# A one-element GpSimd add on the last weight word ahead of its weight sums, and another fixed order list

## The chip, the cores and the metric

The kernel runs on one core of a Trainium2 chip. The metric is the device time of one execution in microseconds (us). Five engines run their own instruction queues side by side: TensorE (PE, matrix products), VectorE (DVE), ScalarE (ACT), GpSimd (POOL) and SyncE (SP, which here only issues DMA transfers). They wait for one another through semaphores.

## The reference, cut to what matters

```python
B, H, S, D = 8, 8, 576, 64          # q and k are scaled by 5.727 and 5.728
scores = 1/np.sqrt(D) * (q_c @ k_c.transpose(...))     # chunks of 64 tokens
attn = softmax(scores, axis=-1)                         # max subtracted, sum + 1e-9
x = (attn @ v_c)  -> [4608 tokens, 512]                 # heads side by side
h = x @ w_in                                            # w_in  [512, 2048]
g = h * (1 / (1 + exp(-1.702 * h)))
out = g @ w_out                                         # w_out [2048, 512]
```

All is float32 in and out, except that the two weights arrive as float64.

## The kernel before

**Tiles.** The 4608 tokens make 36 tiles of 128 rows, and four tiles make one of nine blocks of 512 tokens. The hidden width of 2048 makes 16 slices of 128, each with its own weight word `w_j` (j from 0 to 15), which holds the slice of `w_in` and of `w_out`. A float32 product is made of three matmuls on a high part and a low part of each operand, so each word is kept as two parts, and so are x (`x_h`, `x_l`) and g (`g_h`, `g_l`).

**Weight words.** A word arrives as float64 (`raw_j`, lines 365 and 370: one DMA for `w_in`, one for `w_out`). ACT scales and takes its low bits (`wsc_j` line 374, `wlow_j` line 381), DVE shifts and joins (`wshift_j` line 387, `wj_j` line 394, in a buffer `wtmp` of which there are three), ACT writes the high part (`wh_j`, line 410) and DVE the low part (`w_j`, line 413).

**The plain blocks.** For block n and slice j with g = 16n + j, PE makes the hidden product (`h0_g`, `h_g`, lines 1513 to 1515; for g below 2 in halves, `hh` and `h`, lines 1526 to 1529) into one of two PSUM banks `hp`. ACT takes the gelu (line 1537) and its high part (`gh_g`, line 1538), DVE the low part (`gl_g`, line 1543), which frees the bank. PE then adds four output steps (`o_g_t`, three matmuls each, lines 1553 to 1555). Blocks 0 to 2 run like that.

**The later blocks.** Blocks 3 to 8 go in three pairs by a scheme with seven products in place of eight (`P1` to `P7`, lines 820 to 822). It needs sums of weight words: for each pair p of slices POOL adds the word's two parts (`pa0_p`, `pa_p`: tile `whole`, line 699) and makes four sums of quarters (`psum_p`: tile `sums`, lines 706 to 709). ACT and DVE split these (`phi`, `plo`), a DMA puts them into a DRAM tile `seven` (`pouts`), and the products read them back in pieces (`ld`, lines 807 and 809).

**Attention.** For each tile, or pair of tiles u, PE makes scores (`s_u`), DVE and ACT the softmax, POOL the division (`n_u`, lines 552 and 1323), DVE or PE the transposes (`tq`, `tk`, `et`), and PE the product with v. q and k of the first tiles come by line 470. Tiles 4 and 5 (u = 4) are loaded as `rows`, transposed by PE (line 1259) and copied out by ACT (line 1266) and DVE (line 1269).

**What sets the order.** Every step is entered once with `plan.add`, with its needs. `ORDER` is a fixed list of step names, and `emit` runs the steps in that order, so each engine gets its instructions in the list's order. `need` is only asserted against that list: on the chip an instruction waits for the data and the buffers that it uses, and for nothing else. Before the change `pa0_p` needs `w_15` (`f"w_{NF - 1}"`, NF = 16) in this sense: it stands behind `w_15` in the list, but it reads only the word 2p.

Of the kernel before, what the change touches and what calls it, by code (L numbers as in the profile page):

```python
# [8 lines left out]
F32 = mybir.dt.float32  # L9
# [5 lines left out]
ALU = mybir.AluOpType  # L15
AX = mybir.AxisListType

PE, ACT, DVE, POOL, DMA = "pe", "act", "dve", "pool", "dma"
# [216 lines left out]
def tile_chunk_attention_ffn(  # L235
# [9 lines left out]
    nc = tc.nc  # L245
# [4 lines left out]
    P = 128  # L250
# [3 lines left out]
    NF = DF // P  # L254
# [1381 lines left out]
    def gelu_table():  # L1636
        z = const.tile([P, P], F32, tag="gelu", name="gelu")
        nc.scalar.activation(z[:, :1], ident[:, :1], AF.Gelu_apprx_sigmoid)
# [55 lines left out]
```

## Time and profile before

| what | us |
|---|---|
| median of 3 runs (819.9 to 821.66) | 821.38 |
| the profiled execution | 821.13 |
| its span, first to last instruction | 819.4 |
| outside the span | 1.7 |
| PE busy in the span | 807.3 |
| DVE, ACT, POOL busy | 586.2, 383.5, 91.5 |

The profile was taken on one execution. A timeline row gives the start in us from the span's start, the length in us, the engine, the line, the operation, what it writes and reads, and in brackets the idle time of the engine before it with what ended it. Matmuls are pipelined: a row lasts longer than the distance to the next one.

### The profile page before, as it was taken

The page shows a single profiled execution, that of the slowest core. Times are in us where ns is not written, and L with a number is a line of the kernel's source. Part 1 is how long each engine was busy: PE and PEld are TensorE (multiplying, and loading weights), DVE is VectorE, ACT ScalarE, POOL GpSimd, SP SyncE. Part 2 cuts the span into 40 slices and gives each one's busy share as a digit, 9 for nine tenths or more (in the row PEclk, how much of TensorE's full clock was granted, in tenths as well). Part 3 has the DMA queues.
Part 4 walks back from the last instruction along what each step waited for, and adds up shares of the span by engine and source line. Part 5 has one row for each costly group of instructions (what it writes and reads, how often), then busy time and mean ns, then how long its engine had stood idle before and what let it go on. Part 6 is the DMA issues. An engine that isn't in the chain of part 4 may idle for free.

```text
span 819.4 us, 15635 instructions
## 1 busy us (share of the span) xinstructions
PE 807.3 (99%) x6038; PEld 680.4 (83%) x6038; DVE 586.2 (72%) x865; ACT 383.5 (47%) x603; POOL 91.5 (11%) x82
## 2 busy tenths in 40 slices
PE   7899999999999999999999999999999999999998
PEld 6788878888888888888888888888888888889998
DVE  5788976356475879885698898776887454569852
ACT  5899824244355536423554352422565311267430
POOL 1000170000063661000001010000000000000000
PEclk9999999999999999999999999999999999999999
DMA  9998645353266677767666437686633047673433
GB/s 242 282 297 244 167 129 123 88 128 72 57 182 174 158 199 207 186 173 219 171 172 167 104 92 193 180 211 198 164 104 116 1 130 213 194 207 118 142 92 103
DMA packets 244010, 131.08 MB, mean 160 GB/s; under 512 B 187104, under 2 KB 211680, under 8 KB 243936
## 3 DMA queue, kind: packets, MB, share of 16 engines
q1 hardware_dynamic: 243936, 130.08, 58.6%
q8 instruction: 48, 0.79, 0.4%
q14 instruction: 26, 0.21, 0.1%
HBM read 97.52 MB, written 32.51 MB: 159 GB/s over the span
## 4 chain that ended last, share of the span: by engine, by line
PE 88%; DVE 4%; SPq 3%; ACT 2%; DMA 2%; issue 1%; DVEq 0%; ACTq 0%
PE po L1553 12%; PE po L1555 12%; PE po L1554 12%; PE hp L820 9%; PE hp L822 9%; PE hp L821 9%; PE hp L1515 4%; PE hp L1513 4%; PE hp L1514 4%; SPq L470 2%; PE s L1293 2%; PE x L1367 2%; DMA w<-seven 1%; DVE wtmp L394 1%; PE acc_X L1069 1%; PE acc_X L1068 1%
## 5 line engine op out<-in xcount | busy, mean ns | idle before, releaser
L1553 PE MATMUL po<-w,g_l 128*128 128x512 f32 x448 | 176.8, 395 | 0.6 <-DVE g_l L1543 0.5
L1555 PE MATMUL po<-w,g_h 128*128 128x512 f32 x448 | 174.5, 390 | 0.0
L1554 PE MATMUL po<-w,g_h 128*128 128x512 f32 x448 | 174.5, 389 | 0.0
L1553 PEld LDWEIGHTS po<-w,g_l 128*128 128x128 f32 x448 | 84.1, 188 | 20.1 <-DVE g_l L1543 1.9
L1555 PEld LDWEIGHTS po<-w,g_h 128*128 128x128 f32 x448 | 84.1, 188 | 17.7
L1554 PEld LDWEIGHTS po<-w,g_h 128*128 128x128 f32 x448 | 84.1, 188 | 16.8
L820 PE MATMUL hp<-w,w 128*128 128x512 f32 x224 | 87.6, 391 | 0.3 <-DMA w<-seven 0.2
L1342 DVE STREAM_TRANSPOSE eT<-e 32x512 f32<-32x512 f32 x120 | 84.2, 702 | 4.4 <-POOL e L1323 2.4
L822 PE MATMUL hp<-w,w 128*128 128x512 f32 x224 | 87.2, 389 | 0.0
L821 PE MATMUL hp<-w,w 128*128 128x512 f32 x224 | 87.1, 389 | 0.0
L1323 POOL TENSOR_TENSOR e<-e,r 128x1024 f32<-128x1024 f32 x16 | 31.2, 1953 | 437.8 <-DVE r L1320 365.0
L1513 PE MATMUL hp<-x_l,w 128*128 128x512 f32 x184 | 72.0, 391 | 0.0
L1515 PE MATMUL hp<-x_h,w 128*128 128x512 f32 x184 | 71.6, 389 | 0.0
L1514 PE MATMUL hp<-x_h,w 128*128 128x512 f32 x184 | 71.6, 389 | 0.0
L1543 DVE TENSOR_TENSOR g_l<-hp,g_h 128x512 fp32r<-128x512 f32 (+1 forms) x50 | 33.2, 664 | 51.9 <-ACT g_h L1538 51.8
L1537 ACT ACTIVATE hp<-hp 128x512 f32<-128x512 f32 (+1 forms) x50 | 28.4, 569 | 66.5 <-PE hp L1515 57.3
L820 PEld LDWEIGHTS hp<-w,w 128*128 128x128 f32 x224 | 42.0, 188 | 10.5 <-issue 1.1
L822 PEld LDWEIGHTS hp<-w,w 128*128 128x128 f32 x224 | 42.1, 188 | 8.8
L821 PEld LDWEIGHTS hp<-w,w 128*128 128x128 f32 x224 | 42.1, 188 | 8.6
L820 PE MATMUL hp<-w,pieces 128*128 128x512 f32 x112 | 43.8, 391 | 0.0
L822 PE MATMUL hp<-w,pieces 128*128 128x512 f32 x112 | 43.6, 389 | 0.0
L821 PE MATMUL hp<-w,pieces 128*128 128x512 f32 x112 | 43.6, 389 | 0.0
(237 smaller groups left out, 1558.6 us busy)
## 6 DMA issues: line engine op xcount, KB each, us to landing
w<-seven SPq DMA_DIRECT2D x112, 256.0 KB, 3.3
pieces<-seven SPq DMA_DIRECT2D x56, 256.0 KB, 3.4
seven<-w SPq DMA_DIRECT2D x24, 512.0 KB, 3.8
raw<-in_moe_w_in_dram SPq DMA_DIRECT2D x16, 512.0 KB, 5.9
raw<-in_moe_w_out_dram SPq DMA_DIRECT2D x16, 512.0 KB, 6.3
four<-four_w SPq DMA_DIRECT2D x32, 256.0 KB, 3.2
raw<-in_q_dram SPq DMA_DIRECT2D x208, 32.0 KB, 2.4
raw<-in_k_dram SPq DMA_DIRECT2D x208, 32.0 KB, 2.2
```

What stands on the lines that cost most here:

```text
L820: nc.tensor.matmul(hp, w[:, 0, c], xl[:, c], start=c == 0, stop=False)
L821: nc.tensor.matmul(hp, w[:, 0, c], xh[:, c], start=False, stop=False)
L822: nc.tensor.matmul(hp, w[:, 1, c], xh[:, c], start=False, stop=c == 1)
L1323: nc.gpsimd.tensor_tensor(st["e"], st["e"], bc(st["r"]), op=ALU.mult)
L1342: nc.vector.transpose(st["et"][po : po + 32, :, 32 * a : 32 * a + 32], st["e"][pi : pi + 32, :, 32 * b : 32 * b + 32],)
L1513: nc.tensor.matmul(hp, wh, xl, start=cc == 0, stop=False)
L1514: nc.tensor.matmul(hp, wh, xh, start=False, stop=False)
L1515: nc.tensor.matmul(hp, wl, xh, start=False, stop=cc == NCC - 1)
L1543: nc.vector.tensor_tensor(gl[:, c], hp, gh[:, c].bitcast(F32), op=ALU.subtract)
L1553: nc.tensor.matmul(po, gl[:, c], w[:, 0, :], start=first, stop=False)
L1554: nc.tensor.matmul(po, gh[:, c], w[:, 0, :], start=False, stop=False)
L1555: nc.tensor.matmul(po, gh[:, c], w[:, 1, :], start=False, stop=last)
```

## The change

A new POOL step `gate` adds one element per partition of word 15's low part to itself. The first sums of each pair need `gate` now. And `ORDER` is another list of the same 2693 names and `gate`.

```diff
-        plan.add(POOL, 1.3, rank, lambda: whole(0), need=[w0, f"w_{NF - 1}"], make=e("pa0"), take=["tmp"])
+        plan.add(POOL, 1.3, rank, lambda: whole(0), need=[w0, "gate"], make=e("pa0"), take=["tmp"])
...
+    def gate():
+        t = const.tile([P, 1], F32, tag="gate", name="gate")
+        w = wt[NF - 1][:, 1, 1, :1].bitcast(F32)
+        nc.gpsimd.tensor_tensor(t, w, w, op=ALU.add)
...
+    plan.add(POOL, 0.12, -80, gate, need=[f"w_{NF - 1}"], make="gate")
...
-    "xa_0 xa_1 k_0 k_1 warm q_0 q_1 k_3 tkp_1 q_3 tkp_0 tk_1 tqp_0 tk_0 q_2 tq_0 tqp_1 raw_0 s_0 tq_1 s_1 m_0 k_2 "
```

Since POOL works off its queue in order, all that stands behind `gate` on POOL begins behind word 15's low part. POOL at that place, before (the names are those of above with the word, pair or tile and a buffer number):

```order
L1323 TENSOR_TENSOR e_6_1019<-e_6_1019,r_6_1061 128x1024
L699 TENSOR_TENSOR whole_2_1301<-w_4_664 128x512
L699 TENSOR_TENSOR whole_2_1301<-w_5_716 128x512
L699 TENSOR_TENSOR whole_0_1383<-w_0_289 128x512
L699 TENSOR_TENSOR whole_0_1383<-w_1_448 128x512
L706 TENSOR_TENSOR sums_2_1400<-whole_2_1301 128x256
```

and now:

```order
L1323 TENSOR_TENSOR e_6_1009<-e_6_1009,r_6_1054 128x1024
L1639 TENSOR_TENSOR gate_1318<-w_15_1312 128x1
L699 TENSOR_TENSOR whole_2_1391<-w_4_667 128x512
L699 TENSOR_TENSOR whole_0_1398<-w_0_305 128x512
L699 TENSOR_TENSOR whole_0_1398<-w_1_446 128x512
L699 TENSOR_TENSOR whole_2_1391<-w_5_727 128x512
L706 TENSOR_TENSOR sums_2_1439<-whole_2_1391 128x256
```

The same four adds stand there in another order, with `gate` ahead of them. The sums of pair 0, which stood right behind those of pair 2, now stand behind two divisions (`n_8` and `n_10`).

DVE around the last three words, before (`eT` and `qkT` are transposes of the attention, L387 and L394 shift and join, L413 is the low part of a word, L1543 the low part of g):

```order
L394 ISA wtmp_14_1150<-raw_14_911,wtmp_14_1150 128x2048
L413 TENSOR_TENSOR w_13_1174<-wtmp_13_1140,w_13_1174 128x2x512
L1342 STREAM_TRANSPOSE eT_6_1101<-e_6_1019 32x16x32 x2
L413 TENSOR_TENSOR w_14_1206<-wtmp_14_1150,w_14_1206 128x2x512
L387 TENSOR_SCALAR wtmp_15_1241<-raw_15_1067 128x1024
L1543 TENSOR_TENSOR g_l_12_1224<-hp_12_1186,g_h_12_1223 128x512
L394 ISA wtmp_15_1241<-raw_15_1067,wtmp_15_1241 128x2048
L1342 STREAM_TRANSPOSE eT_6_1101<-e_6_1019 32x16x32 x2
L1277 STREAM_TRANSPOSE qkT_8_1266<-raw_8_965 128x1024 x2
L1543 TENSOR_TENSOR g_l_13_1263<-hp_13_1227,g_h_13_1262 128x512
L413 TENSOR_TENSOR w_15_1253<-wtmp_15_1241,w_15_1253 128x2x512
```

and now:

```order
L413 TENSOR_TENSOR w_13_1187<-wtmp_13_1165,w_13_1187 128x2x512
L1543 TENSOR_TENSOR g_l_12_1212<-hp_12_1189,g_h_12_1211 128x512
L1277 STREAM_TRANSPOSE qkT_8_1225<-raw_8_961 128x1024 x2
L413 TENSOR_TENSOR w_14_1198<-wtmp_14_1093,w_14_1198 128x2x512
L1342 STREAM_TRANSPOSE eT_6_1147<-e_6_1009 32x16x32 x4
L1543 TENSOR_TENSOR g_l_13_1260<-hp_13_1231,g_h_13_1259 128x512
L1342 STREAM_TRANSPOSE eT_6_1147<-e_6_1009 32x16x32 x2
L387 TENSOR_SCALAR wtmp_15_1291<-raw_15_1003 128x1024
L394 ISA wtmp_15_1291<-raw_15_1003,wtmp_15_1291 128x2048
L1543 TENSOR_TENSOR g_l_14_1297<-hp_14_1252,g_h_14_1296 128x512
L413 TENSOR_TENSOR w_15_1312<-wtmp_15_1291,w_15_1312 128x2x512
```

`gl_12` moved ahead of word 14, and `gl_13` ahead of the shift and join of word 15; word 15 itself moved behind more transposes.

SP's queue of DMA issues at the start, before (`first_b` is v of the first four tiles, `rows_4` is q and k of tile 4):

```order
L365 DMA raw_1_237<-in_moe_w_in_dram 128x4x128
L370 DMA raw_1_237<-in_moe_w_out_dram 128x512
L470 DMA rows_4_260<-in_q_dram 128x8x64
L470 DMA rows_4_260<-in_k_dram 128x8x64
L470 DMA first_b_3_245<-in_v_dram 128x8x64
L470 DMA first_b_2_314<-in_v_dram 128x8x64
L365 DMA raw_2_368<-in_moe_w_in_dram 128x4x128
L370 DMA raw_2_368<-in_moe_w_out_dram 128x512
L365 DMA raw_3_385<-in_moe_w_in_dram 128x4x128
L370 DMA raw_3_385<-in_moe_w_out_dram 128x512
```

and now:

```order
L365 DMA raw_1_234<-in_moe_w_in_dram 128x4x128
L370 DMA raw_1_234<-in_moe_w_out_dram 128x512
L470 DMA first_b_2_253<-in_v_dram 128x8x64
L470 DMA first_b_3_250<-in_v_dram 128x8x64
L365 DMA raw_2_327<-in_moe_w_in_dram 128x4x128
L370 DMA raw_2_327<-in_moe_w_out_dram 128x512
L470 DMA rows_4_357<-in_q_dram 128x8x64
L470 DMA rows_4_357<-in_k_dram 128x8x64
L365 DMA raw_3_387<-in_moe_w_in_dram 128x4x128
L370 DMA raw_3_387<-in_moe_w_out_dram 128x512
```

The two loads of tile 4 moved behind word 2; words 1 and 3 kept their places.

## Rows read from the trace of the kernel before

**Rows 1.** The page, part 1: busy us, share of the span and instructions of each engine.

```profile
PE 807.3 (99%) x6038; PEld 680.4 (83%) x6038; DVE 586.2 (72%) x865; ACT 383.5 (47%) x603; POOL 91.5 (11%) x82
```

**Rows 2.** Stretches of 20 us: length, busy time of PE, PEld, DVE, ACT, POOL with instructions, granted clock as a share of 2.4 GHz, DMA share, GB/s.

```profile
0.00:20.00 20.00, 15.26 (x242) 13.30 (x245) 10.54 (x20) 11.00 (x17) 3.45 (x9) 1.00 1.10 241
20.00:40.00 20.00, 16.82 (x255) 14.59 (x247) 15.23 (x24) 17.81 (x28) 1.42 (x2) 1.00 0.97 285
...
100.00:120.00 20.00, 19.49 (x203) 15.49 (x202) 15.76 (x17) 7.54 (x11) 11.89 (x12) 1.00 0.47 137
```

**Rows 3.** PE's timeline in the start: the transposes of tile 4, the hidden product of slice 1's second half, the scores of tile pair 4, the first output step of slice 2.

```profile
31.25 1.03 PE L1259 MATMUL qkTp<-ident,rows 128*128 128x128 f32 x8
...
33.91 0.73 PE L1526 MATMUL hp<-x_h,w 128*128 128x256 f32 x4 [0.68 <-DVE g_l L1543]
...
38.84 1.16 PE L1293 MATMUL s<-qkT 64*64 64x64 f32 x64 [0.97 <-ACT qkT L1266]
...
48.59 0.50 PE L1553 MATMUL po<-w,g_l 128*128 128x512 f32 x1
```

**Rows 4.** SP's timeline: issue of the last part of word 1, of k of tile 4, of the last part of word 2.

```profile
15.05 0.56 SPq L370 DMA_DIRECT2D raw<-in_moe_w_out_dram  x1
...
17.36 0.94 SPq L470 DMA_DIRECT2D rows<-in_k_dram  x1
...
23.82 0.51 SPq L370 DMA_DIRECT2D raw<-in_moe_w_out_dram  x1
```

**Rows 5.** The same three issues in the view of DMA issues: KB, and us from the start of the issue to landing.

```profile
raw<-in_moe_w_out_dram SPq DMA_DIRECT2D x1, 512.0 KB, 6.8
...
rows<-in_k_dram SPq DMA_DIRECT2D x1, 256.0 KB, 6.2
...
raw<-in_moe_w_out_dram SPq DMA_DIRECT2D x1, 512.0 KB, 6.6
```

**Rows 6.** ACT's timeline: scaling of word 2, scaling and low bits of word 3.

```profile
30.50 1.17 ACT L374 ACTIVATE raw<-raw 128x1024 f32<-128x1024 f32 x1 [0.83 <-DMA raw<-in_moe_w_out_dram]
...
33.77 1.17 ACT L374 ACTIVATE raw<-raw 128x1024 f32<-128x1024 f32 x1
34.81 1.18 ACT L381 ACTIVATE raw<-raw 128x1024 int32<-128x1024 uint32 x1
```

**Rows 7.** DVE's timeline: low part of g of slice 0, join of word 3.

```profile
33.43 0.42 DVE L1543 TENSOR_TENSOR g_l<-hp,g_h 128x256 fp32r<-128x256 f32 x1 [1.04 <-ACT g_h L1538]
...
36.33 1.23 DVE L394 CUSTOM_DVE_ANT_0 wtmp<-raw,wtmp 128x2048 uint16<-128x2048 uint16 x1
```

**Rows 8.** PE's timeline from 106 to 121 us: output steps of slices 11 to 13, and the first hidden product of slice 15 (the last row).

```profile
106.22 0.39 PE L1554 MATMUL po<-w,g_h 128*128 128x512 f32 x1
106.44 0.39 PE L1555 MATMUL po<-w,g_h 128*128 128x512 f32 x1
107.02 0.50 PE L1553 MATMUL po<-w,g_l 128*128 128x512 f32 x1 [0.19 <-DVE g_l L1543]
...
112.37 0.39 PE L1555 MATMUL po<-w,g_h 128*128 128x512 f32 x1
113.08 0.50 PE L1553 MATMUL po<-w,g_l 128*128 128x512 f32 x1 [0.32 <-DVE g_l L1543]
...
120.25 0.39 PE L1513 MATMUL hp<-x_l,w 128*128 128x512 f32 x1
```

**Rows 9.** DVE's timeline from 100 to 116 us, in the order of the list above.

```profile
103.53 2.23 DVE L413 TENSOR_TENSOR w<-wtmp,w 128x1024 fp32r<-128x1024 f32 x1
...
106.28 0.68 DVE L1543 TENSOR_TENSOR g_l<-hp,g_h 128x512 fp32r<-128x512 f32 x1
106.88 1.70 DVE L394 CUSTOM_DVE_ANT_0 wtmp<-raw,wtmp 128x2048 uint16<-128x2048 uint16 x1
...
110.08 2.37 DVE L1277 STREAM_TRANSPOSE qkT<-raw 128x1024 f32<-128x1024 f32 x2
112.37 0.65 DVE L1543 TENSOR_TENSOR g_l<-hp,g_h 128x512 fp32r<-128x512 f32 x1
112.95 1.20 DVE L413 TENSOR_TENSOR w<-wtmp,w 128x1024 fp32r<-128x1024 f32 x1
```

**Rows 10.** POOL's timeline: the smallest operation in the trace, the four adds, the first of the four operations of a pair's sums, and the next division behind the sums.

```profile
0.24 0.10 POOL L1676 MEMSET const-float32-0.0<- 128x1 f32 x1 [0.24 <-issue]
...
102.13 2.55 POOL L699 TENSOR_TENSOR whole<-w 128x512 f32<-128x512 f32 x2 [13.39 <-DVE w L413]
105.84 3.90 POOL L699 TENSOR_TENSOR whole<-w 128x512 f32<-128x512 f32 x2 [1.16 <-DVE w L413]
114.32 0.73 POOL L706 TENSOR_TENSOR sums<-whole 128x256 f32<-128x256 f32 x1 [4.58 <-DVE w L413]
...
133.47 1.90 POOL L1323 TENSOR_TENSOR e<-e,r 128x1024 f32<-128x1024 f32 x1 [10.60 <-ACT hp L1537]
```

**Rows 11.** PE's timeline at 548 us, between two products of the seven.

```profile
547.93 0.39 PE L822 MATMUL hp<-w,w 128*128 128x512 f32 x1
548.52 0.47 PE L820 MATMUL hp<-w,w 128*128 128x512 f32 x1 [0.20 <-DMA w<-seven]
```

**Rows 12.** DMA issues from 540 to 549 us: count, KB each, median us from the start of the issue to landing.

```profile
w<-seven SPq DMA_DIRECT2D x3, 256.0 KB, 3.8
...
v<-in_v_dram SPq DMA_DIRECT2D x1, 256.0 KB, 4.8
```

343 rows, old and new, of the table ORDER are left out of this document.

## Prediction

> **What bounds the kernel.** The page's table of engines comes first: PE is busy 807.3 of the span's 819.4 us [rows 1]. No PE instruction is added or taken away, so what can change is the 12.1 us in which PE stands still, and the distances between its matmuls. The view of busy time by stretches of 20 us says where these lie: 4.74 us in the first stretch, 3.18 in the second, 0.51 between 100 and 120 [rows 2]. Most of the rest is the end, where a last result is copied out and stored; the new list ends with the same steps in nearly the same order, so I leave it at nothing. A change of order can therefore win about 8 us at most, nearly all of it in the first 40 us, and can lose whatever new waits it makes. I read the PE timeline in both places, followed each wait back through DVE, ACT and the DMA issues, and then compared the queues of the two lists there.
>
> **Term 1, the start.** PE waits 0.68 us at 33.91, for the low part of g of slice 0, which frees a bank [rows 3]; DVE makes that at 33.43, after 1.04 us of waiting for ACT [rows 7]. ACT stood idle 0.83 us before it scaled word 2 at 30.50 [rows 6], and the gelu is queued behind word 2 there. Word 2's last part is issued at 23.82 and takes 6.6 us, so it lands at 30.42 [rows 4, 5]: the wait is a DMA's. In the new SP queue word 2 stands ahead of tile 4's q and k. Word 1's last part landed at 15.05 + 6.8 = 21.85 and tile 4's k at 17.36 + 6.2 = 23.56 [rows 4, 5], so the two loads took 1.7 us of landing, and word 2 should land near 28.7. ACT is then free at 30.50 - 0.83 = 29.67, the chain runs 0.83 us earlier, and the wait of 0.68 goes. Tile 4's loads now land where word 2 did, near 30.4; the transposes that need them start at 31.25 [rows 3], so 0.85 us of cover is left, and each microsecond beyond it would be PE's.
>
> Most of this is given back. The next wait, 0.97 us at 38.84 [rows 3], is for copies of tile 5, which stand behind the join of word 3 (36.33) on DVE [rows 7]. That join needs word 3's low bits, ready at 34.81 + 1.18 = 35.99 [rows 6], and ACT started on word 3 only when it had landed, a little before 33.77. Word 3 keeps its place in SP's queue, so it lands as before, and the join can move from 36.33 to about 36.05 at best: 0.28 us. Of the 0.68 us some 0.3 us survive at the scores. The third wait, at 48.59, is for g of slice 2, whose chain hangs on these scores; it moves along. **Term 1: -0.3 us.** The ends: -0.6 if that chain gains a further 0.3 us, as it may since its DVE work is ordered differently; +0.3 if tile 4's loads are late by more than their cover, or if the other swaps ahead of 30 us (q before k, v of tile 1 before tile 0) cost something that word 1's landing at 21.85, in the same place in both queues, does not hide.
>
> **Term 2, words 14 and 15.** PE has a gap at 107.02 and one at 113.08, both for a low part of g from DVE. Without a wait a matmul follows the last by 106.44 - 106.22 = 0.22, say 0.23 us [rows 8]. The gaps thus cost 0.58 - 0.23 = 0.35 and 0.71 - 0.23 = 0.48, together 0.83 us, more than the idle time in the brackets says. Why was DVE late? Its low part of word 14 took 2.23 us against 1.20 for word 15's, and the join of word 15 took 1.70 against 1.23 for word 3's [rows 7, 9]. Both stand exactly where POOL runs its four adds, 102.13 to 104.68 and 105.84 to 109.74; the second pair took 3.90 us in place of 2.55 [rows 10]. Word 14's operation ended at 105.76, 1.08 us after POOL's first pair. So whichever of the two began later waited for the other. The g parts, whose input is in PSUM, kept their 0.65 to 0.68 us.
>
> The Trainium skill, "SBUF — State Buffer", section "Who interferes with whom", says the same as a rule: a DVE instruction with two SBUF inputs and a GpSimd instruction that reads SBUF block one another whole, and issue order decides who waits. By it word 14 would end at 104.68 + 1.20 = 105.88 (an estimate); the row says 105.76, so the trace agrees.
>
> `gate` keeps POOL off until word 15 is done, and what follows on DVE (low parts of x, maxima, differences, low parts of g) has not two SBUF inputs of full size. The new list also takes the low part of slice 12 ahead of word 14, and that of slice 13 ahead of word 15's join: in the old list the latter stood behind that join and behind 2.37 us of transposes at 110.08 [rows 9]. Counting in durations of rows, slice 12's part is then due some 0.6 us before PE asks for it, and slice 13's more than 1 us. **Term 2: -0.83 us**, with the ends 0 (DVE is as late for another reason) and -0.83.
>
> **Term 3, what the gate costs.** No such add is in the trace. The smallest POOL operation takes 0.10 us, an operation of 256 columns 0.73 [rows 10]; I take 0.2, nearer to the small one, as one column is. It is paid on POOL alone, which had 10.60 us idle before the division at 133.47 [rows 10]. Behind the gate stand four adds (2 x 2.55 = 5.1 us) and the sums (4 x 0.73 = 2.9): from word 15's end, put at 116 since it moved behind more transposes, POOL is done at 116 + 0.2 + 5.1 + 2.9 = 124.2, 9 us before that division. The sums waited for word 15 before already (4.58 us at 114.32). Word 15 itself is asked for by PE at 120.25, less the 1.1 us won [rows 8]: 3 us of cover, and if it were gone each microsecond would be PE's. **Term 3: 0.** The ends are 0 and 0.73.
>
> **Term 4, the rest.** From 120 us on the list is reshuffled everywhere, and PE is full. Before there are two more gaps, at 548.52, where a piece of the seven products came late (0.59 - 0.23 = 0.36 us [rows 11]), and one of about 0.3 at 716. I take nothing for the rest: one list has about as many tight places as the other.
>
> **Sum.** 821.13 (the profiled execution) - 0.3 - 0.83 = 820.0. That execution lies 0.25 us under the median of 821.38, so against the median I predict 821.38 - 1.13 = **820.2 us**, 0.14% less. A measurement of this kernel can tell about 0.2% (1.6 us) from no change.
>
> **Rivals.** (a) *All gaps close*: the start gives 0.6, words 14 and 15 give 0.83, and the two late gaps (0.36 and 0.3) do not come back: 821.38 - 2.1 = 819.3, faster by 0.25%. For it: the late gaps hang on one order each. Against it: another order has its own. (b) *The gate does not do what it says for PE*: POOL no longer blocks word 14, but the new DVE order is as late in another place before 116 us (word 7 or slice 9 have, counted as above, only some 0.3 us of cover), so only term 1 is left: 821.1, no change. (c) *Slower, by pieces that come late*: a product asks for its piece 4.08 us of PE work (three products of six matmuls, 18 x 0.227) or less after the list issues it nine times in the new list, seven times in the old. While loads of v and others pass, a piece or v took 3.8 to 4.8 us to land [rows 12], and the one gap cost 0.36. If all nine pay that, 9 x 0.36 = 3.2 us are lost: 821.38 - 1.13 + 3.2 = 823.5. It decides from the point at which a landing takes longer than 4.08 us. Against it: of the seven in the old list one paid.
>
> **How the numbers follow.** The forecast has 0.44, (a) 0.27, (b) 0.16, (c) 0.13. Faster by over 0.2% (under 819.74): (a) and 0.03 of the forecast's lower edge, 0.30. Slower by over 0.2% (over 823.0): (c), 0.13. Within: 0.57. The range of 819.0 to 822.2 holds the forecast with its ends (-1.43 to 0), (b) and nearly all of (a), and part of the way to (c); it leaves out (c) and some of (a), about 0.17.
>
> **What would show it.** In the new profile: word 2's scaling begins before 30 us and no PE wait of 0.68 is left near 34; a wait for the copies of tile 5 is still there, near 38.5; POOL's first adds begin behind word 15, at 114 to 117; no low part of a word from 100 to 116 takes over 1.3 us; no PE gap is named between 100 and 120; the division that stood at 133.47 is not late. Wrong would be a PE wait of over 0.5 us behind 50 us, a scaling of word 2 that still waits at 30 us, or low parts of words at 2 us although POOL rests.

## The result, and the profile after

The changed kernel takes 829.8 us (median of 5 runs, 829.2 to 831.88), the kernel before 821.63 in the same comparison (819.9 to 822.85): a ratio of 1.0104, interval 1.0086 to 1.0123. That is 8.2 us more, far outside the range of the prediction. The profiled execution has a span of 828.0 us, 8.6 more than before.

The engines' line of the page, to be read beside [rows 1]:

```profile
PE 817.9 (99%) x6038; PEld 681.3 (82%) x6038; DVE 586.7 (71%) x865; ACT 381.1 (46%) x603; POOL 91.2 (11%) x83
```

PE stood still for 828.0 - 817.9 = 10.1 us, 2.0 less than before. But it was busy 10.6 us longer with the same 6038 instructions at the same clock. There are gains in the foreseen places; something else costs 10 us, and it is inside the matmuls' own pace.

The gains first. Stretches of 20 us (columns as in [rows 2]):

```profile
0.00:20.00 20.00, 15.58 (x250) 13.40 (x250) 9.79 (x19) 10.87 (x17) 3.36 (x9) 1.00 1.04 235
20.00:40.00 20.00, 17.61 (x235) 15.80 (x236) 16.45 (x26) 18.45 (x30) 2.19 (x2) 1.00 1.01 288
...
100.00:120.00 20.00, 20.00 (x206) 16.33 (x205) 14.59 (x19) 5.69 (x9) 3.88 (x5) 1.00 0.48 124
```

Idle time in the first 40 us fell from 7.92 to 6.81 us, and from 100 to 120 us from 0.51 to nothing. ACT's timeline has the scaling of word 2 ([rows 6]), PE's the scores of tile pair 4 ([rows 3]):

```profile
29.54 1.17 ACT L374 ACTIVATE raw<-raw 128x1024 f32<-128x1024 f32 x1
```

```profile
38.15 1.16 PE L1293 MATMUL s<-qkT 64*64 64x64 f32 x64 [1.09 <-ACT qkT L1266]
```

Word 2 is scaled 0.96 us earlier and waits for nothing; PE's wait of 0.68 us is gone, and the next one, for the copies of tile 5, is still there. DVE's timeline around words 14 and 15 ([rows 9]) and POOL's ([rows 10]):

```profile
105.48 1.18 DVE L413 TENSOR_TENSOR w<-wtmp,w 128x1024 fp32r<-128x1024 f32 x1
...
112.46 1.23 DVE L394 CUSTOM_DVE_ANT_0 wtmp<-raw,wtmp 128x2048 uint16<-128x2048 uint16 x1
...
114.82 1.22 DVE L413 TENSOR_TENSOR w<-wtmp,w 128x1024 fp32r<-128x1024 f32 x1 [0.53 <-ACT w L410]
```

```profile
116.12 0.19 POOL L1639 TENSOR_TENSOR gate<-w 128x1 f32<-128x1 f32 x1 [27.73 <-DVE w L413]
116.27 5.04 POOL L699 TENSOR_TENSOR whole<-w 128x512 f32<-128x512 f32 x4
...
123.58 0.74 POOL L709 TENSOR_TENSOR sums<-whole,sums 128x256 f32<-128x256 f32 x1
```

Neither DVE's words nor POOL's adds are stretched any more, and the gate takes 0.19 us. Now the pace. PE's timeline in the middle of the plain blocks, the first and last of eleven matmuls in a row of output steps, before:

```profile
153.57 0.39 PE L1553 MATMUL po<-w,g_l 128*128 128x512 f32 x1
...
155.84 0.39 PE L1554 MATMUL po<-w,g_h 128*128 128x512 f32 x1
```

and after:

```profile
153.25 0.39 PE L1553 MATMUL po<-w,g_l 128*128 128x512 f32 x1
...
155.58 0.40 PE L1554 MATMUL po<-w,g_h 128*128 128x512 f32 x1
```

Ten distances take 2.27 us before and 2.33 after: 0.227 and 0.233 from one matmul to the next. No row says that PE waited. This goes on from 28 to 739 us, for the output steps and for the products with `pieces`, 3 x 448 and 3 x 112 matmuls: on the mean of the trace 0.2328 us in place of 0.2271, together 9.4 us. The products between them are slower too, by less. Six hidden products behind one another, with the matmul that follows them, before:

```profile
150.85 0.39 PE L1513 MATMUL hp<-x_l,w 128*128 128x512 f32 x1
...
152.21 0.39 PE L1513 MATMUL hp<-x_l,w 128*128 128x512 f32 x1
```

and after, between two output steps:

```profile
149.10 0.39 PE L1513 MATMUL hp<-x_l,w 128*128 128x512 f32 x1
...
150.49 0.39 PE L1553 MATMUL po<-w,g_l 128*128 128x512 f32 x1
```

They take 1.39 us in place of 1.36. All such products of 512 columns took 0.2289 us on the mean of the trace in place of 0.2269, some 2.4 us more. The two groups lose about 11.8 us; the gaps that were won bring this down to the 8.6 us by which the span grew.

### The profile page after: what moved, and what is told of

The parts are those of the page before. It is cut to its first block, busy times and chain, and to the rows that moved or that the text cites. A ratio compares the mean times of both kernels' runs of the same rounds, so it can differ in the third digit from the quotient of the medians.

```text
span 828.0 us, 15637 instructions
## 1 busy us (share of the span) xinstructions
PE 817.9 (99%) x6038; PEld 681.3 (82%) x6038; DVE 586.7 (71%) x865; ACT 381.1 (46%) x603; POOL 91.2 (11%) x83
## 4 chain that ended last, share of the span: by engine, by line
PE 96%; DVE 2%; ACT 1%; DMA 0%; issue 0%; POOL 0%; SPq 0%; POOLq 0%; DVEq 0%
PE po L1553 13%; PE po L1555 12%; PE po L1554 12%; PE hp L822 9%; PE hp L820 9%; PE hp L821 9%; PE hp L1515 5%; PE hp L1513 5%; PE hp L1514 5%; PE s L1293 2%; PE x L1367 2%; PE acc_X L1069 1%; PE acc_Y L1069 1%; PE acc_X L1067 1%; PE acc_X L1068 1%; PE acc_Y L1067 1%
## 5 line engine op out<-in xcount | busy, mean ns | idle before, releaser
L1553 PE MATMUL po<-w,g_l 128*128 128x512 f32 x448 | 178.9, 399 | 0.0
L1555 PE MATMUL po<-w,g_h 128*128 128x512 f32 x448 | 177.2, 396 | 0.0
L1554 PE MATMUL po<-w,g_h 128*128 128x512 f32 x448 | 176.8, 395 | 0.0
L1543 DVE TENSOR_TENSOR g_l<-hp,g_h 128x512 fp32r<-128x512 f32 (+1 forms) x50 | 33.3, 666 | 50.8 <-ACT g_h L1538 50.4
L820 PEld LDWEIGHTS hp<-w,w 128*128 128x128 f32 x224 | 42.0, 188 | 10.1 <-DVE g L801 0.6
L822 PE MATMUL hp<-w,pieces 128*128 128x512 f32 x112 | 44.3, 396 | 0.0
L821 PE MATMUL hp<-w,pieces 128*128 128x512 f32 x112 | 44.3, 395 | 0.0
L820 PE MATMUL hp<-w,pieces 128*128 128x512 f32 x112 | 44.2, 395 | 0.0
```

The source lines that it names most:

```text
L820: nc.tensor.matmul(hp, w[:, 0, c], xl[:, c], start=c == 0, stop=False)
L821: nc.tensor.matmul(hp, w[:, 0, c], xh[:, c], start=False, stop=False)
L822: nc.tensor.matmul(hp, w[:, 1, c], xh[:, c], start=False, stop=c == 1)
L1543: nc.vector.tensor_tensor(gl[:, c], hp, gh[:, c].bitcast(F32), op=ALU.subtract)
L1553: nc.tensor.matmul(po, gl[:, c], w[:, 0, :], start=first, stop=False)
L1554: nc.tensor.matmul(po, gh[:, c], w[:, 0, :], start=False, stop=False)
```

## The experiments

What could slow these matmuls? The output steps and the products with `pieces`, which lose most, have their stationary operand in a buffer that **moved**. The gate's tile takes 32 bytes of each partition's memory, and stands right behind x, the weight words and the attention's large tiles. What lies behind it is shifted by 32 bytes, exactly or but for multiples of 512: `sA`, `sB` (which holds `pieces`), the gelu table's tile, the small softmax tiles, `g_h`, `g_l`, the output buffers and `wtmp`. `g_h`, for one, begins at byte 203424 in place of 203392. What lies ahead of it kept its offset to multiples of 512, which is 128 for the start of every tile that a matmul reads in the kernel before. The **address theory** says that this costs the time; the **list theory**, that the new order does; the **gate theory**, that the added GpSimd instruction does. Each ratio below is against runs of the kernel before on the same chip, with its 95% interval.

**1. Gate tile of 64 bytes.**

```diff
-        t = const.tile([P, 1], F32, tag="gate", name="gate")
+        t = const.tile([P, 16], F32, tag="gate", name="gate")
...
```

> Address theory: the 4-byte gate tile takes 32 bytes, so every buffer behind it begins 32 bytes past a multiple of 64, and matmuls that use these buffers come slower one behind the other (about 10 us in all, against 2 us less of PE idle time). With a gate tile of 64 bytes these buffers are at multiples of 64 again: 819 to 820.5 us. List theory: the same list, so the same time as after, 829 to 830.5. Gate theory (the added GpSimd instruction itself disturbs): also 829 to 830.5.

Measured: 830.38 us, ratio 1.0112 (1.0098 to 1.0126). A miss for the address theory as I had put it: multiples of 64 do not help.

**2. Old list, no gate, the same buffers shifted by 32 bytes.**

```diff
-        z = const.tile([P, P], F32, tag="gelu", name="gelu")
+        z = const.tile([P, P + 8], F32, tag="gelu", name="gelu")
```

> Address theory: the old list and no gate, but with the unused tail of the gelu table's tile 32 bytes longer, so that the same buffers are shifted by 32 bytes: 829 to 832 us, with the spacing of the output matmuls at 0.232 us in place of 0.227. List theory and gate theory: 821 to 822, as before.

Measured: 831.93 us, ratio 1.0136 (1.0121 to 1.0152). Eight unused elements in the kernel before cost more than the whole change. The list and the gate theories fall as the cause of the loss.

**3. New list without the gate and its tile.**

```diff
...
-        plan.add(POOL, 1.3, rank, lambda: whole(0), need=[w0, "gate"], make=e("pa0"), take=["tmp"])
+        plan.add(POOL, 1.3, rank, lambda: whole(0), need=[w0, f"w_{NF - 1}"], make=e("pa0"), take=["tmp"])
...
-    plan.add(POOL, 0.12, -80, gate, need=[f"w_{NF - 1}"], make="gate")
```

> The new list without the gate step and its tile; the buffers are where they were before. Address theory: 819.5 to 821 us; POOL's four adds can meet DVE's last words again, so up to 0.8 us more than with an aligned gate. List theory: 829 to 831. Gate theory: 819.5 to 821.

Measured: 819.96 us, ratio 0.9988 (0.9979 to 0.9997). The list itself is good. DVE's low parts of words 14 and 15, and POOL's first adds, in this kernel:

```profile
104.97 1.18 DVE L413 TENSOR_TENSOR w<-wtmp,w 128x1024 fp32r<-128x1024 f32 x1
...
114.31 1.23 DVE L413 TENSOR_TENSOR w<-wtmp,w 128x1024 fp32r<-128x1024 f32 x1 [0.53 <-ACT w L410]
```

```profile
100.06 1.29 POOL L699 TENSOR_TENSOR whole<-w 128x512 f32<-128x512 f32 x1 [11.54 <-DVE w L413]
106.30 3.78 POOL L699 TENSOR_TENSOR whole<-w 128x512 f32<-128x512 f32 x3 [4.94 <-DVE w L413]
```

POOL adds between DVE's two words here, and neither word is blocked: for these gaps the new list does not need the gate.

**4. Old list with the gate, tile of 64 bytes.** The steps of the change's diff, `gate` behind `w_15` in the old `ORDER`.

> The old list with the gate behind word 15, its tile 64 bytes: what the gate gives by itself. Term 2 of the prediction holds for the gate alone: the low part of word 14 takes 1.2 us in place of 2.2, and PE's gaps near 107 and 113 us go: 820.6 to 821.2. If the two gaps came from the order of DVE's steps and not from POOL: 821.4 to 822. Gate theory: 828 to 830.

Measured: 831.34 us, ratio 1.0127 (1.0113 to 1.0141). The address effect buries what was asked of the time; number 8 asks again. The trace does answer for the operation: word 14's low part took 1.22 us, against 2.23 in number 2 with the same list and no gate.

**5. Gate tile of 128 bytes** (`[P, 32]` in the new list).

> The new list with its gate, the gate tile 128 bytes, so that the buffers behind it keep their offset to multiples of 128. If 128 is the grain that matters: 819 to 820.5 us, the output matmuls back at a spacing of 0.227. If any move of these buffers harms, or the gate itself does: 829 to 831, as with 4 and 64 bytes.

Measured: 828.97 us, ratio 1.0104 (1.0088 to 1.0119). A miss again: 128 bytes are as bad as 32.

**6. Only `sA` and `sB` shifted, by 32 bytes**: the gate's 4-byte tile, and the tile behind `sB` shorter by as much.

```diff
-        z = const.tile([P, P], F32, tag="gelu", name="gelu")
+        z = const.tile([P, P - 8], F32, tag="gelu", name="gelu")
```

> The new list with the 4-byte gate tile, and the gelu table's tile 32 bytes shorter: only the tiles sA, sB (pieces of the seven products) and gelu are shifted by 32 bytes, the g tiles are not. If the price is one of each matmul whose stationary operand is shifted: some 340 matmuls with pieces x 0.006 = 2 us, so 821 to 822.5 us, with the spacing at 0.233 for pieces and 0.227 for g. If the tiles of g and the temporaries make none of it: 829 or more. If the gate instruction does: 829 or more.

Measured: 821.99 us, ratio 1.0013 (1.0004 to 1.0022). PE's timeline, first and last of twelve output matmuls, and of twelve with `pieces`:

```profile
151.46 0.39 PE L1553 MATMUL po<-w,g_l 128*128 128x512 f32 x1
...
153.95 0.39 PE L1555 MATMUL po<-w,g_h 128*128 128x512 f32 x1
```

```profile
320.17 0.39 PE L820 MATMUL hp<-w,pieces 128*128 128x512 f32 x1
...
322.74 0.40 PE L822 MATMUL hp<-w,pieces 128*128 128x512 f32 x1
```

Eleven distances take 2.49 us (0.226 each) with g in its old place, 2.57 (0.234) with pieces shifted.

**7. The other half: g, softmax tiles and temporaries shifted**, `sA` and `sB` not (the diff of number 2, in the new list without gate; there the gelu table's tile stands behind `sB`, in the old list ahead of `sA`).

> The new list without gate, and the gelu table's tile 32 bytes longer: the g tiles, the small softmax tiles and the temporaries are shifted by 32 bytes, sA and sB are not. If the price is one of each matmul with a shifted stationary operand: some 1300 to 1500 output matmuls x 0.0057 = 7.4 to 8.6 us on 820: 827 to 829, spacing 0.233 for g and 0.228 for pieces. If it is one of the pieces: 820.

Measured: 827.99 us, ratio 1.0090 (1.0076 to 1.0103). The same two stretches:

```profile
152.90 0.39 PE L1553 MATMUL po<-w,g_l 128*128 128x512 f32 x1
...
155.46 0.40 PE L1555 MATMUL po<-w,g_h 128*128 128x512 f32 x1
```

```profile
324.18 0.39 PE L820 MATMUL hp<-w,pieces 128*128 128x512 f32 x1
...
326.68 0.39 PE L822 MATMUL hp<-w,pieces 128*128 128x512 f32 x1
```

Now the output steps take 2.56 and the pieces 2.50. Against the new list at the old places (0.9988) number 6 costs 0.25% (2.1 us) and number 7 1.02% (8.4 us); together 10.5, about the 9.5 us between 0.9988 and the 1.0104 of the change. So the price goes mainly with the place of a matmul's own operands: where only `sA` and `sB` moved, the output steps keep their pace. That ACT, DVE and DMA, which use the same buffers, are not the cause is shown by the next runs.

**Matmuls alone.** To find the rule I measured runs of 96 matmuls (three accumulated per bank, 128 x 128 by 512) with chosen byte offsets of the stationary and the moving operand past a multiple of 128; both tiles begin at a multiple of 512 plus 128.

> Leaves out the whole computation: matmuls of 128 x 128 by 512 alone on the core, 96 in a row for each of 15 pairs of byte offsets (stationary operand, moving operand) past a multiple of 128. If a shifted stationary operand costs each matmul some 6 ns by itself: 0.233 us from one to the next at stationary offsets of 16, 32, 64 and 96, and 0.227 at 0 and 128 whatever the moving operand does. If it is the moving operand's offset: the other way round. If the price only exists beside the other engines' traffic: 0.227 or less in all.

Measured, as the time between the first matmuls of successive runs over 96: 0.2267 to 0.2272 us at the offsets (stationary, moving) = (0, 0), (16, 0), (32, 32) and (64, 64); 0.233 at (32, 0), (64, 0), (0, 32), (0, 96), (0, 128); 0.2341, 0.2322, 0.2316 and 0.2289 at (96, 0), (128, 0), (0, 16) and (0, 64). None of the three expectations holds: not one operand's place counts, but the **distance** between the two. Shift both alike, and the price is gone; and it needs no other engine's traffic. Two pairs do not fit a plain rule: (16, 0) costs nothing, and (0, 64) 2 ns in place of 6. Each kernel of matmuls alone was run once.

A second such kernel asks for the grain; its line for the pair (256, 0):

```diff
+    for i in range(96): nc.tensor.matmul(bank[i // 3 % 4], at(st, 256, P, i % 4), at(mv, 0, 512), start=i % 3 == 0, stop=i % 3 == 2)
```

> Leaves out the whole computation: 96 matmuls in a row for each of 18 pairs of byte offsets (stationary, moving). Distance theory with a grain of 512: 0.2267 us from one to the next at 512 and 1024 for either operand and at (128, 128), 0.232 to 0.235 at 256 and 384. With a larger grain: slow at 512 too. A distance of 16 was fast for the stationary operand and slow for the moving one; 8, 16 and the pairs (32, 48) and (48, 32) show whether the sign counts.

PE's timeline of this kernel, one row for each pair: lines 32 to 35 are (0, 0), (256, 0), (384, 0), (512, 0); 37 to 39 (0, 256), (0, 384), (0, 512); 41 to 43 (128, 128), (16, 0), (0, 16); 45 to 47 (0, 8), (32, 48), (48, 32).

```profile
26.51 21.92 PE L32 MATMUL bank<-moving,stationary 128*128 128x512 f32 x96
48.27 21.93 PE L33 MATMUL bank<-moving,stationary 128*128 128x512 f32 x96
70.04 22.48 PE L34 MATMUL bank<-moving,stationary 128*128 128x512 f32 x96
92.36 21.95 PE L35 MATMUL bank<-moving,stationary 128*128 128x512 f32 x96
...
135.91 21.92 PE L37 MATMUL bank<-moving,stationary 128*128 128x512 f32 x96
157.67 22.55 PE L38 MATMUL bank<-moving,stationary 128*128 128x512 f32 x96
180.06 21.94 PE L39 MATMUL bank<-moving,stationary 128*128 128x512 f32 x96
...
223.60 21.93 PE L41 MATMUL bank<-moving,stationary 128*128 128x512 f32 x96
245.36 22.56 PE L42 MATMUL bank<-moving,stationary 128*128 128x512 f32 x96
267.76 22.41 PE L43 MATMUL bank<-moving,stationary 128*128 128x512 f32 x96
...
312.16 22.57 PE L45 MATMUL bank<-moving,stationary 128*128 128x512 f32 x96
334.57 22.40 PE L46 MATMUL bank<-moving,stationary 128*128 128x512 f32 x96
356.80 21.94 PE L47 MATMUL bank<-moving,stationary 128*128 128x512 f32 x96
```

The second column divides them: 21.92 to 21.95 at every distance that is a multiple of 256 (1024 too, which is not shown), 22.3 to 22.6 else. The expected grain of 512 was a miss: 256 is enough. One distance does not fit: +16 (stationary less moving) is long on line 42, short on line 47 and in the run before this one.

**8. Gate tile of 512 bytes, new list; and the old list with such a gate.** The shifted buffers keep a multiple of 512 to the weight words.

> The new list with its gate, the gate tile 512 bytes, so that the shifted buffers keep their distance to the weight words as a multiple of 512. Distance theory (a matmul is slowed where stationary and moving operand differ in their address by no multiple of 512): 819 to 820.3 us, spacing of the output matmuls 0.227. If any move of these buffers harms: 829 to 831.

> The old list with the gate behind word 15, its tile 512 bytes. Distance theory, with term 2 of the prediction: the two gaps near 107 and 113 us go, 0.83 us less than before: 820.0 to 821.0. Without term 2: as before. If any move of the buffers harms: 829 to 831.

Measured: 819.57 us, ratio 0.9988 (0.9977 to 0.9999), for the new list; 819.97, ratio 0.9986 (0.9977 to 0.9996), for the old one. The output matmuls of the new list:

```profile
152.15 0.39 PE L1553 MATMUL po<-w,g_l 128*128 128x512 f32 x1
...
154.64 0.39 PE L1555 MATMUL po<-w,g_h 128*128 128x512 f32 x1
```

2.49 us again. And the old list's low parts of words 14 and 15 with the gate:

```profile
104.88 1.23 DVE L413 TENSOR_TENSOR w<-wtmp,w 128x1024 fp32r<-128x1024 f32 x1
...
112.81 1.21 DVE L413 TENSOR_TENSOR w<-wtmp,w 128x1024 fp32r<-128x1024 f32 x1
```

1.23 and 1.21 us in place of 2.23 and 1.20 ([rows 9]), and no PE gap between 90 and 130 us.

**9. All tiles shifted alike by 32 bytes** (the 4-byte gate tile allocated ahead of all others).

```diff
+    gate_out = const.tile([P, 1], F32, tag="gate", name="gate")
     ident = const.tile([P, P], F32, tag="ident", name="ident")
...
```

> The changed kernel with its 4-byte gate tile allocated ahead of all other tiles, so that every tile is shifted by 32 bytes alike. Distance theory: the distances are as before, so 819 to 820.3 us. If the address of an operand itself has to be at its old place to a multiple of 512: 830 or more, since now x and the weight words are shifted too.

Measured: 821.87 us, ratio 1.0014 (1.0005 to 1.0022). The loss of 10 us is gone, so it is the distance and not the address; but 2 us remain over number 8, and the expected range was missed. The view of waits of this kernel, of one execution, has:

```profile
PE hp L821 <- DMA w<-seven: 2.8, 2, 1.8
```

In the changed kernel PE waits 0.2 us for such loads, in number 8 0.7. Whether the loads were late because of the shift was not tried.

**10. The gate's 4-byte tile behind all others; a gate tile of 256 bytes.**

```diff
+    late = ctx.enter_context(tc.tile_pool(name="late", bufs=1))
...
-        t = const.tile([P, 1], F32, tag="gate", name="gate")
+        t = late.tile([P, 1], F32, tag="gate", name="gate")
```

> The changed kernel with its 4-byte gate tile behind all other tiles, so that every buffer is where it was before. If only the places of the buffers cost the 10 us: 819 to 820.3 us, as with a gate tile of 512 bytes; the sum of the prediction (820.2) is then right for the list and the gate. If a 4-byte write of GpSimd harms: 829.

> The new list, the gate tile 256 bytes. If the grain of the distance is 256, as with matmuls alone: 819 to 820.3 us. If it is 512 beside the other engines: 829 to 831.

Measured: 820.58 us, ratio 0.9999 (0.9986 to 1.0011), with every buffer at its old place or a multiple of 512 from it, just above the expected 820.3; 819.69 us, ratio 0.9985 (0.9974 to 0.9996), with 256 bytes. The grain in the kernel is 256, as with matmuls alone. The first of the two scattered from 818.8 to 823.5 us, as did the kernel before on that chip (819.7 to 823.5); the mean of the three ratios of the new list with its gate at harmless places (0.9988, 0.9999, 0.9985) is 0.9991.

**11. Mixed places, and fewer columns.**

> Leaves out the whole computation: 96 matmuls in a row for each of 16 patterns. Stationary offsets 0 0 0 32 32 32: if a matmul's own distance counts, the time from a matmul at 32 to the next is 0.233 and from one at 0 it is 0.227, whatever follows; if the next one's stationary operand counts (loaded while this one runs), the time before a matmul at 32 is long. Offset 16 three times behind different rows: 0.2267 or 0.233 each time, if what ran before decides. With 256 and 128 columns: the same 6 ns at a distance of 32 if the price is one of each matmul, 3 and 1.5 ns if it is one of the columns.

PE's timeline: line 33 has the stationary operand at 0 and 32 in turn; 36, 38 and 40 have it at 16, behind runs at (0, 0), (32, 0) and (0, 16); 42 and 43 are (0, 0) and (32, 0) with 256 columns, 44 and 45 the same with 128.

```profile
50.24 22.72 PE L33 MATMUL bank<-moving,stationary 128*128 128x512 f32 x96
...
116.78 21.93 PE L36 MATMUL bank<-moving,stationary 128*128 128x512 f32 x96
...
160.94 22.56 PE L38 MATMUL bank<-moving,stationary 128*128 128x512 f32 x96
...
205.59 21.93 PE L40 MATMUL bank<-moving,stationary 128*128 128x512 f32 x96
...
249.12 11.67 PE L42 MATMUL bank<-moving,stationary 128*128 128x256 f32 x96
260.63 11.51 PE L43 MATMUL bank<-moving,stationary 128*128 128x256 f32 x96
271.98 10.83 PE L44 MATMUL bank<-moving,stationary 128*128 128x128 f32 x96
282.65 10.88 PE L45 MATMUL bank<-moving,stationary 128*128 128x128 f32 x96
```

Neither of the two simple readings holds. With 0 0 0 32 32 32 (line 32) a matmul at 32 took 0.233 us to the next one at 32 and 0.236 to one at 0, one at 0 took 0.229 to one at 32 and 0.228 to the next at 0: both count, which agrees with the slower products beside the moved ones in the changed kernel. On line 33, where the place changes each time, the distances are 0.232 to 0.240, on the mean 0.235. The offset of 16 is short behind (0, 0), long behind (32, 0), and short behind (0, 16), which was itself long (line 39, not shown): there what ran before decides, by no rule that these runs show. With 256 columns nothing is lost (11.35 us for 96 at 32, 11.51 at 0, from the starts), and with 128 next to nothing (10.72 and 10.67): of these three widths the price was seen at 512 columns only.

## Why the prediction was wrong

**The step that failed** stands in its first paragraph: no PE instruction is added, so what can change is the idle time "and the distances between its matmuls". The distances were named and then priced nowhere: a change of order "can lose whatever new waits it makes", and nothing else. Term 3 asked what the gate costs as an instruction (0.2 us on POOL, measured 0.19, and hidden as it said), not what its *tile* costs: 32 bytes that move all buffers behind it. Term 4 took nothing for the rest, and looked for it in waits only. The 10 us lie in no wait: they are 6 ns more on each of some 1680 matmuls, and some 2 us on the products between them. No rival had them either; the slower one, late pieces, was not it (0.2 us of such waits after, as before). Nor did the three signs of being wrong catch it: none of them appeared, since all three were waits or stretched operations.

Could the trace of before have told? It holds no matmul with such a distance: all tiles that PE reads there begin at one and the same offset to a multiple of 512. What could have been seen is that the change adds a tile in the middle of the memory, and that its 4 bytes move the operands of the busiest engine. The Trainium skill, "SBUF — State Buffer", section "Who interferes with whom", gives PE two read ports, one for the moving operand and one for the weight load, and calls them independent. Read alone, that lets no price be expected from the operands' places; the runs of matmuls alone show one: 0.2267 us at distance 0, 0.233 at 32, with no other engine at work.

**The rest of the sum came out right, in part by luck.** With the buffers at harmless places the list and the gate give ratios of 0.9988, 0.9985 and 0.9999, where the prediction's 820.2 over 821.38 is 0.9986. Below that total two terms were off in opposite ways: PE's idle time in the start mostly fell by more than term 1 had, and term 4, put at nothing, lost to late pieces.

- *Term 1, the start (-0.3, ends -0.6 and +0.3).* The foreseen waits behave as forecast: the one of 0.68 us goes, the one behind it stays (1.09 us after, 1.77 in number 8). But the first is missing in number 2 as well, which has the old list and no gate: there word 2 is scaled at 29.79, after a wait of 0.16 us for its DMA in place of 0.83. So the swap of the loads is not shown to be what removed it: with the old order of loads word 2 could start 0.7 us earlier too. The size was too small: PE's idle time in the first 40 us fell by 1.1 us in the changed kernel, by 0.4 in number 8 (new list), and by 0.2 to 1.1 in all ten kernels with the new list, in eight of them by more than the end of 0.6 (in number 2 by 0.7).
- *Term 2, words 14 and 15 (-0.83).* Right: both gaps are gone in every kernel with the gate or the new list. The stretched operation depends on the gate in the old list: word 14's low part took 2.23 us again in number 2, without the gate, and 1.22 in number 4, with it. The old list with the gate alone gains 0.14% (1.1 us; 0.3 to 1.9 by its interval). What the prediction did not separate: list and gate each do it, and the second adds nothing that was measured (0.9988 without the gate, 0.9991 in the mean with it).
- *Term 3.* The time on POOL was right (done with the first sums at 124.3, forecast 124.2); the price of the tile was missing.
- *Term 4.* No new wait of over 0.5 us in the changed kernel behind 50 us; in other executions of the new list single waits of 0.5 to 1.0 us turn up there (pieces, once a low part of g), and of up to 1.8 us in number 9. That is the kind of loss that the rival of late pieces had; put at nothing, it took back some 0.5 to 0.7 us in the profiled executions of number 8 (new list) and number 10.

**What stays open.** Why the distance counts, and why only with 512 columns; why +16 depends on what ran before; why the old list lost more from a shift (1.36%) than the new one (1.16%); and the 2 us of number 9. In the traces the old list's larger loss is not in PE's pace: added up over 0.2267 us for each, the distances come to 12.7 us in number 2 and to 12.8 in the changed kernel.

## What to carry to other kernels

A diff that adds a small buffer moves every buffer behind it: compare the two programs' allocations before the costs of their instructions. Where matmuls of 512 columns (float32r, as here) run back to back, keep the stationary and the moving operand a multiple of 256 bytes apart, or put small tiles behind the large ones; here that was worth 10 us of 820. A loss without waits, spread over one engine at an unchanged clock, points to the operands of its instructions and not to the order. And a wait for a DMA that was read from one execution can be missing in the next one of the same list, as the 0.68 us are in number 2.

## What was not expected of the hardware

PE's pace depends on the distance in bytes between its two operands in a partition: 96 matmuls of 128 x 128 by 512 took 21.92 to 21.95 us at multiples of 256, and 22.3 to 22.6 us at nearly all others, with no other engine at work (lines 41 and 38 of the second kernel of matmuls alone: 21.93 and 22.55). The exceptions are +16, which was short or long by what ran before, and -64, which cost 2 ns each in place of 6. Matmuls beside slowed ones pay a part (0.2289 us in place of 0.2269 in the changed kernel). At 256 columns no difference was seen (11.51 us for 96 at distance 0, 11.35 at 32).
